# Expert layers of a fused attention, MoE and MLP kernel: 512-token slots with the second matmul two steps behind the first

## The chip, the cores and the metric

The kernel runs on one core of one Trainium2 chip. The metric is the device time of one execution in microseconds. The kernel before takes 896.44 us, the median of three runs (895.2, 896.44 and 897.1 us).

## The reference

Three layers follow one another. A gated linear attention gives 3072 tokens of 384 numbers. A mixture of experts sends each token to one of 8 experts (384 to 1024 to 384, ReLU) and scales the result by the gate weight. An MLP follows (384 to 2048 to 384, squared ReLU).

```python
# attention, for each step t
state = alpha[:, :, t, :, None] * state + einsum('bhd,bhe->bhde', k[:, :, t], v[:, :, t])
y[:, :, t] = einsum('bhd,bhde->bhe', q[:, :, t], state)
# experts; x is y as (3072, 384)
logits = x @ w_gate + modality_bias[modality_id]
e_idx = argmax(logits, axis=1)
gate_w = softmax(logits)[arange(N), e_idx]
for e in range(8):
    mask = e_idx == e
    out[mask] = gate_w[mask, None] * (maximum(x[mask] @ w1[e], 0) @ w2[e])
# MLP
r = maximum(x @ w_in, 0)
out = (r * r) @ w_out
```

All data are float32. With the reference's inputs (seed 0) two of the experts get all tokens, 1512 and 1560.

## The kernel before

**Stages.** The attention runs over 24 tiles of 128 tokens and takes the first 205 us of the span. The gate's logits, ranks and counts are computed beside it, and the scaled tokens go to DRAM (`xs`). Then come the expert layers in *slots*: a slot is 256 tokens of one expert, gathered from `xs` by an indirect DMA on GpSimd (POOL). The kernel has 13 slots, numbered 0 to 12. Slots 0 and 1 belong to the expert that leads after 16 tiles (the early slots); their token lists are ready before the others, so they cover the computing of the rest. The last stage is the MLP, in six chunks of 512 tokens and 16 steps each; it begins at 475 us.

**One matmul in three.** Every float32 product is made from three matmuls of a rounded high part and a low part (`mm3`). So every operand is split: `split` casts the high part on ScalarE (ACT, line 480) and subtracts it on VectorE (DVE, line 481). This holds for the weights, for x and for the hidden values.

```python
def mm3(o, ah, al, bh, bl, start, stop):
    PE.matmul(o, ah, bh, start=start, stop=False)
    PE.matmul(o, ah, bl, start=False, stop=False)
    PE.matmul(o, al, bh, start=False, stop=stop)
```

**A slot.** `gather` loads the tokens as two blocks of 128 rows (`xg`). `x_T` transposes them on TensorE (PE) into a PSUM tile `xt` (pool `ps_x`, one buffer) and splits that into `xh` and `xl`. `mm1(i, f)` makes one of eight 128-column blocks of the hidden layer: 9 matmuls into `hps`, then `hh` by a ReLU on ACT (line 582) and `hl` on DVE (line 583). After all eight, `mm2(i, d)` makes one of three output blocks `oo` with 24 matmuls each, and `mm2_out` copies the result into `x2T`, at an offset that is read from a register.

**Weights.** `wload` queues seven pieces of an expert: three of w1 (512 KB) and four of w2 (384 KB). At most four are in flight. `pop()` splits the oldest piece and issues the next one. There are two sets of split weights. In the loop over slots `pop()` stands behind `mm1` of f = 1, 3 and 6 and four times around `mm2`.

**w_in and w_out.** They arrive as 64-bit numbers and are converted in 24 pieces: `conv_load` (SyncE, SP), `conv_v` (five instructions on DVE, one on ACT), `conv_g` (two on POOL), `conv_store`. Pieces 0 to 11 run in the attention, 12 to 23 in slots 1 to 12, one each (two loads in slot 1).

**What sets the order.** The scheduler is off. Each engine executes in the order in which the program is written, and waits where a tile isn't ready or a buffer isn't free. An instruction that waits holds everything behind it on its engine.

**Slot assignment.** `finalize_a`, `finalize_h` and `finalize_b` compute on DVE, from the counts, the expert of each slot (`ej_i`), the place of each token (`hr`, and from it the lists `ids`) and the offsets (`eo_i`). If the slots don't suffice (`nsl_i` over `NMAIN`), the program runs a second, general path at its end (`general`), which computes everything again tile by tile.

Of the kernel before, what the change touches and what calls it, by code (L numbers as in the profile page):

```python
# [54 lines left out]
def body(ctx, tc, qka, v, alpha, mod, wg, mbias, w1, w2, w_in, w_out, out):  # L55
# [16 lines left out]
    xctx = ctx.enter_context(ExitStack())  # L72

# [11 lines left out]
    pbuf = dram.tile([NT + SL], I32, name="pbuf")  # L85
# [61 lines left out]
    ones8 = gc.tile([128, NREST], F32, name="ones8")  # L147
# [13 lines left out]
    ej_i = const.tile([128, NREST], I32, name="ej_i")  # L161
    eo_i = const.tile([128, NREST], I32, name="eo_i")
# [3 lines left out]
    def setup_gate():  # L166
# [5 lines left out]
        iota_f("slj", [128, NREST], [[1, NREST]], 0, 0)  # L172
# [5 lines left out]
        SY.dma_start(pbuf.rearrange("(o n) -> o n", n=C), raz[0][:(NT + SL) // C, 0, :C].bitcast(I32))  # L178
# [58 lines left out]
    def gate_c(g):  # L237
# [10 lines left out]
        V.tensor_scalar(rhx_all[:, t0:t0 + T, :], ri, 7, 1, op0=ALU.logical_shift_right, op1=ALU.bitwise_xor)  # L248
# [537 lines left out]
    for i in range(1, NS):  # L786
# [31 lines left out]
        if i == 1:  # L818
            x_T(i + 1, 0)
# [301 lines left out]
```

## Time and profile before

| | us |
|---|---|
| median of three runs | 896.44 |
| lowest and highest run | 895.2 and 897.1 |
| span of the profiled execution, first to last instruction | 888.7 |
| slot 2 to the end of slot 12 (251.5 to 475.2 in the span) | 223.6 |
| PE busy, share of the span | 836.7, 94% |
| VectorE busy | 551.4, 62% |
| ScalarE busy | 409.2, 46% |
| GpSimd busy | 195.3, 22% |

One execution was profiled; of its own time the span is known, 888.7 us, which is 7.7 us under the median of the runs. Rows of the profile give busy times, and the idle time of an engine with what ended it. Matmuls overlap, so the length of one (0.28 us at 256 columns) is more than the spacing of two (0.12 us); a busy PE can still be slowed. The granted clock of TensorE stands in a column of its own, 1.00 for 2.4 GHz and 0.50 for 1.2 GHz.

### The profile page before, as it was taken

Reading aid. Unit: us, or ns where it says so; the run is one execution under the profiler, and the core shown is the slowest. Engines: PE = TensorE matmul, PEld = TensorE weight load, DVE = VectorE, ACT = ScalarE, POOL = GpSimd, SP = SyncE. Lnnn points to the kernel's source line nnn. Section 1 sums busy time; section 2 is a strip of 40 time slices with the busy share of each in tenths; the row PEclk is TensorE's granted clock in tenths of the full one; section 3 lists DMA queues with packets and bytes.
Section 4 is the critical chain, followed back from the end, with each engine's and each line's share of the span. In section 5 each row is a group of like instructions: output and inputs, shape, how many; then the busy total and the mean of one; then the engine's idle time right before and its main releaser. Section 6 shows DMA issues by size and latency. Waiting matters only on the chain.

```text
span 888.7 us, 14046 instructions
## 1 busy us (share of the span) xinstructions
PE 836.7 (94%) x5424; PEld 776.9 (87%) x5424; DVE 551.4 (62%) x878; ACT 409.2 (46%) x746; POOL 195.3 (22%) x179
## 2 busy tenths in 40 slices
PE   7998889798999998989999999999999999999995
PEld 6988778698998888988988999989999999999985
DVE  7999999877577766776768634445445433333340
ACT  3655465495265554655546524324324233333331
POOL 6445355234222232322111000000000000100001
PEclk7878689699999999999999999999999999999998
DMA  9665384362496899789876300300300000000001
GB/s 247 193 195 183 114 284 145 101 224 86 130 262 212 212 210 199 204 195 196 202 199 192 104 1 18 113 1 18 112 1 19 19 1 11 26 1 18 19 1 39
DMA packets 50227, 104.59 MB, mean 118 GB/s; under 512 B 11773, under 2 KB 32279, under 8 KB 50151
## 3 DMA queue, kind: packets, MB, share of 16 engines
q1 hardware_dynamic: 46951, 93.77, 39.0%
q0 software_dynamic: 3200, 9.83, 3.1%
q8 instruction: 44, 0.72, 0.3%
q14 instruction: 32, 0.26, 0.1%
HBM read 87.83 MB, written 15.76 MB: 117 GB/s over the span
## 4 chain that ended last, share of the span: by engine, by line
PE 62%; DVE 18%; DMA 12%; issue 3%; ACT 3%; SPq 0%; POOL 0%; POOLq 0%; DVEq 0%; ACTq 0%
DMA raw<-w_dram 10%; PE h L558 8%; PE acc L559 8%; PE h L559 7%; PE acc L557 7%; PE acc L558 7%; PE h L557 7%; DVE acum L386 3%; PE oo L558 2%; PE oo L559 2%; DVE rs L390 2%; PE oo L557 2%; PE sp L412 2%; PE y L468 2%; DVE kt L394 2%
## 5 line engine op out<-in xcount | busy, mean ns | idle before, releaser
L852 DVE TENSOR_TENSOR r<-r 128x512 f32<-128x512 f32 x96 | 66.5, 693 | 147.8 <-ACT r L851 147.6
L851 ACT ACTIVATE r<-h 128x512 f32<-128x512 f32 x96 | 57.4, 598 | 160.8 <-PE h L559 159.6
L559 PE MATMUL acc<-w2h,hl 128*128 128x384 f32 x376 | 126.9, 338 | 0.0
L557 PE MATMUL acc<-w2h,hh 128*128 128x384 f32 x376 | 126.6, 337 | 0.0
L558 PE MATMUL acc<-w2l,hh 128*128 128x384 f32 x376 | 126.3, 336 | 0.0
L558 PE MATMUL h<-xl,w1h 128*128 128x512 f32 x288 | 113.9, 395 | 0.8 <-DVE xl L481 0.8
L559 PE MATMUL h<-xh,w1l 128*128 128x512 f32 x288 | 113.9, 395 | 0.0
L557 PE MATMUL h<-xh,w1h 128*128 128x512 f32 x288 | 112.1, 389 | 0.0
L875 POOL DMA_INDIRECT out_dram<-ob,pidx x24 | 24.0, 999 | 380.0 <-ACT ob L873 341.1
L481 DVE TENSOR_TENSOR hl<-r,hh 128x512 fp32r<-128x512 f32 x94 | 65.0, 692 | 64.5 <-ACT hh L480 34.3
L557 PE MATMUL oo<-hh,w2h 128*128 128x256 f32 x312 | 92.1, 295 | 7.9 <-ACT hh L582 7.9
L558 PE MATMUL oo<-hl,w2h 128*128 128x256 f32 x312 | 91.5, 293 | 7.4 <-DVE hl L583 7.3
L557 PE MATMUL hps<-xh,w1h 128*128 128x256 f32 x312 | 90.4, 290 | 3.3 <-DVE hl L583 3.3
L480 ACT CAST hh<-r 128x512 fp32r<-128x512 f32 x94 | 58.3, 620 | 75.7 <-DVE r L852 75.7
L559 PE MATMUL oo<-hh,w2l 128*128 128x256 f32 x312 | 90.4, 290 | 0.0
L558 PE MATMUL hps<-xl,w1h 128*128 128x256 f32 x312 | 88.4, 283 | 0.1
L559 PE MATMUL hps<-xh,w1l 128*128 128x256 f32 x312 | 88.2, 283 | 0.0
L481 DVE TENSOR_TENSOR w1l<-raw,w1h 128x1024 fp32r<-128x1024 f32 x42 | 51.2, 1222 | 47.5 <-ACT w1h L480 46.8
L557 PEld LDWEIGHTS acc<-w2h,hh 128*128 128x128 f32 x376 | 70.7, 188 | 4.1
L558 PEld LDWEIGHTS acc<-w2l,hh 128*128 128x128 f32 x376 | 70.6, 188 | 4.0
L559 PEld LDWEIGHTS acc<-w2h,hl 128*128 128x128 f32 x376 | 70.5, 188 | 0.2 <-DVE hl L481 0.2
L557 PEld LDWEIGHTS oo<-hh,w2h 128*128 128x128 f32 x312 | 62.0, 199 | 9.3 <-ACT hh L582 9.3
(194 smaller groups left out, 1768.1 us busy)
## 6 DMA issues: line engine op xcount, KB each, us to landing
raw<-w_dram SPq DMA_DIRECT2D x36, 512.0 KB, 10.5
raw<-w_dram SPq DMA_DIRECT2D x48, 384.0 KB, 5.7
qk<-qka_dram SPq DMA_DIRECT2D x23, 675.5 KB, 5.6
raw<-w_in_dram SPq DMA_DIRECT2D x12, 512.0 KB, 5.8
cvr<-w_out_dram SPq DMA_DIRECT2D x12, 512.0 KB, 9.7
vv<-v_dram SPq DMA_DIRECT2D x24, 192.0 KB, 5.0
xs<-xb SPq DMA_DIRECT2D x24, 192.0 KB, 3.0
alr<-alpha_dram SPq DMA_DIRECT2D x9, 512.0 KB, 4.5
```

What stands on the lines that cost most here:

```text
L386: V.tensor_tensor_scan(acum.rearrange("p a c -> p (a c)"), al, one0.rearrange("p a c -> p (a c)"), 0.0, op0=ALU.mult, op1=ALU.max)
L390: V.tensor_tensor_scan(rs.rearrange("p a c -> p (a c)")[:, ::-1], al[:, ::-1], rz.rearrange("p a c -> p (a c)")[:, ::-1], 0.0, op0=ALU.mul ...
L394: V.tensor_tensor(kt, kk, rs[:, :, 2:], op=ALU.mult)
L412: PE.matmul(sp[:, 2 * p:2 * p + 2, :], pr["kt"][:, 2 * g + p, :], pr["qb"][:, 2 * g + p], start=True, stop=True)
L480: A.copy(hi, raw)
L481: V.tensor_sub(lo, raw, hi)
L557: PE.matmul(o, ah, bh, start=start, stop=False)
L558: PE.matmul(o, ah, bl, start=False, stop=False)
L559: PE.matmul(o, al, bh, start=False, stop=stop)
L851: A.activation(r, o, AF.Relu)
L852: V.tensor_mul(r, r, r)
L875: G.indirect_dma_start(out=out, out_offset=bass.IndirectOffsetOnAxis(ap=pidx[:, n:n + 1], axis=0), in_=ob, in_offset=None)
```

## The change

Slots 0 and 1 keep 256 tokens. Slots 2 to 6 have 512 tokens, slot 7 has 256; there are 8 slots instead of 13, for the same 3328 places. An expert's remaining tokens are counted in units of 256; the first expert with an odd count has its last unit in slot 7. `x_T1` transposes one block of 128 features of a slot (four transposes for 512 tokens). `s1` and `s2` replace `mm1` and `mm2` in slots 2 to 7: step f does the first matmul of block f and the second matmul of block f - 2, which adds to three accumulators that stay open over the slot. Steps 6 and 7 of the second matmul run in the next slot. `pop()` stands behind `s1` in steps 1 to 7. Two pieces of w_out are converted in each of slots 2 to 7. `xg` has one buffer of four blocks instead of two of two, `hh` and `hl` have four buffers instead of five.

```diff
-NREST = REST // SL + NE - 1
-NMAIN = REST // SL + 1
-HC = 2 * NREST
+HC = 4 * NBIG + 2
+NSLOT = NBIG + 3
...
     def finalize_a():
...
+        V.tensor_scalar(ui, cnt, float(SL - 1), 0.0, op0=ALU.add, op1=ALU.max)
+        V.tensor_single_scalar(ui, ui, 8, op=ALU.logical_shift_right)
...
+        V.tensor_single_scalar(ui, ui, 1, op=ALU.bitwise_and)
...
+        V.scalar_tensor_tensor(small, nodd, 1.0, odd, op0=ALU.is_equal, op1=ALU.mult)
...
+        V.tensor_add(nb, u, odd)
+        V.scalar_tensor_tensor(nb, nb, 0.5, small, op0=ALU.mult, op1=ALU.subtract)
...
     def finalize_h():
...
+        V.scalar_tensor_tensor(sel, rk_all, ts, sel, op0=ALU.is_ge, op1=ALU.mult)
+        V.scalar_tensor_tensor(hr, sel, dsum, hr, op0=ALU.mult, op1=ALU.add)
         fin["hr"] = hr
...
+    def blocks(i):
+        return 2 if i < 2 or i == NSLOT - 1 else 4
...
     def gather(i):
         si = slot_ids(i)
-        xg = xp.tile([128, 2, DM], F32, tag="xg", name="xg")
-        for hf in range(2):
+        xg = xp.tile([128, 4, DM], F32, tag="xg", name="xg", bufs=1)
+        for hf in range(blocks(i)):
...
+    def x_T1(i, k):
+        n = blocks(i) * 128
+        xt = ps_x.tile([128, 512], F32, tag="x", name="xt")
+        for hf in range(blocks(i)):
+            PE.transpose(xt[:, hf * 128:(hf + 1) * 128], xgs[i][:, hf, k * 128:(k + 1) * 128], ident)
...
+        split(xt[:, :n], xh[:, :n], xl[:, :n])
...
-        pools["hp"] = pool(mctx, "hp", 5)
...
+        pools["hp"] = pool(mctx, "hp", 4)
...
+    pools["o3"] = pool(octx, "ps_o3", 1, PSUM, side="right")
...
+    drain(("w1", 0))
+    perm(1, offset(1))
+    gather(2)
+    for f in range(4, 8):
+        mm1(1, f)
+        if f == 6:
+            pop()
+    drain(("w2", 0))
+    pop()
+    mm2(1, 0)
+    pop()
+    x_T1(2, 0)
+    mm2(1, 1)
+    mm2_out(1, offset(1), 0, 2)
+    x_T1(2, 1)
+    pop()
+    mm2(1, 2)
+    x_T1(2, 2)
...
+    def s1(i, f):
...
+        for k in range(KD):
+            mm3(o, w[0][:, k, fs], w[1][:, k, fs], *xxs[i][k], k == 0, k == KD - 1)
...
+        A.activation(hh, o, AF.Relu)
+        V.scalar_tensor_tensor(hl, o, 0.0, hh, op0=ALU.max, op1=ALU.subtract)
...
+    def s2(i, f):
...
+        for d in range(KD):
+            dsl = slice(d * 128, (d + 1) * 128)
+            mm3(sac[i][d][:, :n], w[0][:, f, dsl], w[1][:, f, dsl], hh, hl, f == 0, f == 7)
+        if f == 7:
+            for d in range(KD):
+                A.copy(pools["x2T"][:, d, ds(soff[i], n)], sac[i][d][:, :n])
...
+    for i in range(2, NSLOT):
+        last = i == NSLOT - 1
+        cv = 8 + 2 * i
+        for f in range(8):
+            if f == 0:
+                if i > 2:
+                    s2(i - 1, 6)
...
+                else:
+                    gather(i + 1)
+                    push(wload(i))
+            s1(i, f)
+            if f == 1:
+                conv_load(cv)
+            if f == 2:
+                conv_load(cv + 1)
+            if f in (3, 5):
+                conv_v(cv + f // 4)
+                conv_g(cv + f // 4)
...
             if f > 0:
                 pop()
+            if f == 5:
+                if last:
+                    xx2[0] = xsplit(chunks[0], range(1))
+                else:
+                    x_T1(i + 1, 0)
+            if f == 7:
+                if last:
+                    xx2[0] = xsplit(chunks[0], range(1, KD), xx2[0])
+                else:
+                    x_T1(i + 1, 1)
+            if f == 1 and i > 2:
+                s2(i - 1, 7)
+            if f >= 2:
+                s2(i, f - 2)
+            if f == 7 and not last:
+                x_T1(i + 1, 2)
```

ACT before, from the first transposes of the next slot to the conversion in the second matmul (`hh` and `xh` are as above, `w1h` the high part of w1, `raw` a landed piece; DMAHW4 and so on are DMA completions):

```order
L480 CAST xh<-xt 128x512 [waits PE_49]
L582 ACTIVATE hh<-hps 128x256 [waits DVE_49,PE_49]
L480 CAST w1h_171<-raw 128x1024 [waits DMAHW4_49]
L582 ACTIVATE hh<-hps 128x256 [waits PE_49]
L480 CAST w1h_171<-raw 128x1024 [waits DMAHW5_49]
L480 CAST xh<-xt 128x256 [waits PE_49]
L480 CAST w1h_171<-raw 128x1024 [waits DMAHW6_49]
L627 ACTIVATE cvr<-cvr 128x512 [waits Pool_49]
```

ACT after, in slot 2, steps 3 to 5 (`cvr` is a piece of w_out):

```order
L880 ACTIVATE hh<-hps 128x512 [waits DVE_49,PE_49]
L689 ACTIVATE cvr<-cvr 128x512 [waits DMAHW0_49]
L529 CAST w1h_171<-raw 128x1024 [waits DMAHW6_49]
L880 ACTIVATE hh<-hps 128x512 [waits DVE_49,PE_49]
L529 CAST w1h_171<-raw 128x1024 [waits DMAHW7_49]
L880 ACTIVATE hh<-hps 128x512 [waits DVE_49,PE_49]
L689 ACTIVATE cvr<-cvr 128x512 [waits DMAHW2_49]
L529 CAST w1h_171<-raw 128x1024 [waits DMAHW1_49]
L529 CAST xh<-xt 128x512 [waits PE_49]
```

The casts of w1 stood around the ReLU of the last block, which the second matmul of the whole slot needs. Now each stands behind the ReLU of its own step.

PE before, in a slot, the two places where the next slot's tokens are transposed, blocks 0 and 1 of 128 features together in the first matmul, block 2 in the second one:

```order
L559 MATMUL hps<-xh,w1l_2729 128x256
L550 MATMUL xt<-ident,xg 128x128 [waits DMASW6_49,PE_49]
L550 MATMUL xt<-ident,xg 128x128 [waits DMASW7_49]
L550 MATMUL xt<-ident,xg 128x128 x2
L557 MATMUL hps<-xh,w1h_2728 128x256 [waits DVE_49]
...
L559 MATMUL oo<-hh,w2l_2731 128x256
L550 MATMUL xt<-ident,xg 128x128 [waits PE_49]
L550 MATMUL xt<-ident,xg 128x128
L557 MATMUL oo<-hh,w2h_2730 128x256
L558 MATMUL oo<-hl,w2h_2730 128x256
```

PE after, the end of a slot, from the last first-matmul of the slot to behind the transposes of block 2:

```order
L621 MATMUL hps<-xh,w1l_2765 128x512
L612 MATMUL xt<-ident,xg 128x128 [waits DVE_49]
L612 MATMUL xt<-ident,xg 128x128 x3
L619 MATMUL oo<-hh,w2h_2766 128x512 [waits Activation_49]
L620 MATMUL oo<-hl,w2h_2766 128x512
L621 MATMUL oo<-hh,w2l_2767 128x512
...
L612 MATMUL xt<-ident,xg 128x128 [waits DVE_49]
L612 MATMUL xt<-ident,xg 128x128 x3
L619 MATMUL oo<-hh,w2h_2766 128x512 [waits Activation_49]
```

The transposes of blocks 1 and 2 stood 42 matmuls apart (blocks 0 and 1 shared one tile); they now have nine matmuls between them and use the same PSUM tile.

DVE after, the last steps of the same slot (`w2l` is the low part of w2):

```order
L688 TENSOR_SCALAR cvt<-cvr 128x512 [waits DVE_49]
L530 TENSOR_TENSOR w1l_172<-raw,w1h_171 128x1024 [waits DMAHW1_49,Activation_49]
L530 TENSOR_TENSOR xl<-xt,xh 128x512 [waits Activation_49]
L881 SCALAR_TENSOR_TENSOR hl<-hps,hh 128x512 [waits Activation_49]
L530 TENSOR_TENSOR w2l_174<-raw,w2h_173 128x768 [waits DMAHW3_49,Activation_49]
L881 SCALAR_TENSOR_TENSOR hl<-hps,hh 128x512 [waits Activation_49]
L530 TENSOR_TENSOR w2l_174<-raw,w2h_173 128x768 [waits DMAHW4_49,Activation_49]
L530 TENSOR_TENSOR xl<-xt,xh 128x512 [waits Activation_49] x2
L881 SCALAR_TENSOR_TENSOR hl<-hps,hh 128x512 [waits Activation_49] x2
```

The `xl` of blocks 1 and 2 now stand together at the end, behind the `hl` and the w2 split of the last step.

## Rows read from the trace of the kernel before

**Rows 1.** Page, chain that ended last: shares of the span by line.
```profile
DMA raw<-w_dram 10%; PE h L558 8%; PE acc L559 8%; PE h L559 7%; PE acc L557 7%; PE acc L558 7%; PE h L557 7%; DVE acum L386 3%; PE oo L558 2%; PE oo L559 2%; DVE rs L390 2%; PE oo L557 2%; PE sp L412 2%; PE y L468 2%; DVE kt L394 2%
```

**Rows 2.** Windows: from:to length, busy of PE PEld DVE ACT POOL (xcount), PEclk, DMA share, GB/s.
```profile
251.54:475.16 223.62, 206.94 (x1648) 202.54 (x1647) 157.42 (x243) 124.23 (x220) 58.27 (x40) 0.98 0.85 207
```

**Rows 3.** Windows, three 256-token slots of the kernel before, in order.
```profile
311.10:331.80 20.70, 18.50 (x152) 18.09 (x152) 14.28 (x23) 11.39 (x20) 6.33 (x5) 1.00 0.95 212
331.80:354.60 22.80, 19.86 (x152) 19.46 (x151) 14.33 (x23) 11.41 (x20) 6.22 (x5) 0.93 0.91 202
354.60:372.80 18.20, 18.20 (x153) 18.08 (x152) 13.88 (x22) 11.26 (x20) 5.18 (x5) 1.00 0.86 227
```

**Rows 4.** Timeline, PE, the second of these slots: start, length, engine, line, operation [idle before].
```profile
345.45 0.38 PE L557 MATMUL oo<-hh,w2h 128*128 128x256 f32 x1 [2.01 <-ACT hh L582]
346.76 0.39 PE L558 MATMUL oo<-hl,w2h 128*128 128x256 f32 x1 [0.93 <-DVE hl L583]
```

**Rows 5.** Windows, just behind these two waits.
```profile
348.00:351.00 3.00, 3.00 (x16) 3.00 (x16) 1.67 (x3) 1.65 (x2) 0.00 (x0) 0.50 1.02 375
```

**Rows 6.** Timeline, ACT, the same place.
```profile
344.07 1.04 ACT L480 CAST w1h<-raw 128x1024 fp32r<-128x1024 f32 x1 [3.80 <-DMA raw<-w_dram]
```

**Rows 7.** Page, DMA issues: KB each, median us from issue to landing.
```profile
raw<-w_dram SPq DMA_DIRECT2D x36, 512.0 KB, 10.5
...
cvr<-w_out_dram SPq DMA_DIRECT2D x12, 512.0 KB, 9.7
...
xg<-xs,ids_b POOLq DMA_INDIRECT x2, 3.0
```

**Rows 8.** Timeline, PE: first and last of 27 unbroken 256-column matmuls.
```profile
290.42 0.28 PE L557 MATMUL hps<-xh,w1h 128*128 128x256 f32 x1
...
293.54 0.28 PE L559 MATMUL hps<-xh,w1l 128*128 128x256 f32 x1
```

**Rows 9.** Timeline, PE: nine 512-column matmuls in the last stage, first and last.
```profile
489.07 0.39 PE L557 MATMUL h<-xh,w1h 128*128 128x512 f32 x1
...
490.92 0.39 PE L559 MATMUL h<-xh,w1l 128*128 128x512 f32 x1
```

**Rows 10.** Timeline, PE, slot 1: an output block starts; later four transposes between matmuls.
```profile
245.21 0.28 PE L557 MATMUL oo<-hh,w2h 128*128 128x256 f32 x1
...
248.09 0.60 PE L550 MATMUL xt<-ident,xg 128*128 128x128 f32 x4
248.44 0.36 PE L557 MATMUL oo<-hh,w2h 128*128 128x256 f32 x1
```

**Rows 11.** Groups by line and form: xcount | busy us, mean ns.
```profile
L481 DVE TENSOR_TENSOR w2l<-raw,w2h 128x768 fp32r<-128x768 f32 x56 | 60.6, 1088 | 14.7 <-ACT w2h L480 14.4
...
L851 ACT ACTIVATE r<-h 128x512 f32<-128x512 f32 x96 | 57.4, 598 | 160.8 <-PE h L559 159.6 <-DMA wo<-cvt 0.3
...
L481 DVE TENSOR_TENSOR w1l<-raw,w1h 128x1024 fp32r<-128x1024 f32 x42 | 51.2, 1222 | 47.5 <-ACT w1h L480 46.8 <-issue 0.5
...
L481 DVE TENSOR_TENSOR xl<-xt,xh 128x512 fp32r<-128x512 f32 x13 | 9.0, 690 | 4.0 <-ACT xh L480 3.7 <-issue 0.2
```

**Rows 12.** Timeline, DVE: first and last of the five instructions of one conversion.
```profile
247.38 0.42 DVE L622 TENSOR_SCALAR cvt<-cvr 128x512 int32<-128x512 int32 x1
...
249.49 0.43 DVE L626 TENSOR_SCALAR cvt<-cvr 128x512 int32<-128x512 int32 x1
```

**Rows 13.** Timeline, DVE: a small instruction of the slot assignment, and what follows the last.
```profile
225.69 0.17 DVE L329 TENSOR_TENSOR sb<-sb,noh 128x8 f32<-128x8 f32 x1
...
230.30 0.69 DVE L481 TENSOR_TENSOR xl<-xt,xh 128x512 fp32r<-128x512 f32 x1 [1.79 <-ACT xh L480]
```

**Rows 14.** Timeline, POOL: the fourth gather behind the finished token lists.
```profile
243.25 1.59 POOL L542 DMA_INDIRECT xg<-xs,ids  x1 [0.30 <-issue]
```

**Rows 15.** Line 542, gathers started from 242 to 245 us.
```profile
DMA to landing us min/median/max: 6.2/6.9/7.7
```

**Rows 16.** Timeline, PE: where the second step of the last stage starts.
```profile
478.57 0.39 PE L557 MATMUL h<-xh,w1h 128*128 128x512 f32 x1
```

More of the change, by code (lines that the diff above doesn't have):

```diff
@@ L84, in body @@
     xs = dram.tile([NT, DM], F32, name="xs")
[L85 removed]
+    pbuf = dram.tile([NT + PAD], I32, name="pbuf")
     wi32 = dram.tile([DM, FF2], F32, name="wi32")
@@ L145, in iota_f @@
         iot[name] = f
-    ones8 = gc.tile([128, NREST], F32, name="ones8")
+    ones8 = gc.tile([128, NBIG + 1], F32, name="ones8")
     lbias = gc.tile([128, NTILE, NE], F32, name="lbias")
@@ L328, in finalize_a, with t8 @@
-        V.tensor_sub(sb, sbi, nsm)
+        def t8(tag, shape=NE, dt=F32):
+            return fp.tile([128, shape], dt, tag="f_" + tag, name=tag)
+        cnt = t8("cnt")
+        V.scalar_tensor_tensor(cnt, ohs, -2.0 * SL, run, op0=ALU.mult, op1=ALU.add)
+        ui = t8("ui", dt=I32)
+        V.tensor_scalar(ui, cnt, float(SL - 1), 0.0, op0=ALU.add, op1=ALU.max)
+        V.tensor_single_scalar(ui, ui, 8, op=ALU.logical_shift_right)
+        u = t8("u")
+        V.tensor_copy(u, ui)
+        V.tensor_single_scalar(ui, ui, 1, op=ALU.bitwise_and)
@@ new lines, in finalize_a @@
+        odd = t8("odd")
+        V.tensor_copy(odd, ui)
+        nodd = t8("nodd")
+        V.tensor_tensor_scan(nodd, ones8[:, :1].to_broadcast([128, NE]), odd, 0.0, op0=ALU.mult, op1=ALU.add)
+        small = t8("small")
+        V.scalar_tensor_tensor(small, nodd, 1.0, odd, op0=ALU.is_equal, op1=ALU.mult)
+        nb = t8("nb")
+        V.tensor_add(nb, u, odd)
+        V.scalar_tensor_tensor(nb, nb, 0.5, small, op0=ALU.mult, op1=ALU.subtract)
+        nbm = t8("nbm")
+        V.tensor_mul(nbm, nb, noh)
@@ L601, in offset @@
         if i < 2:
-            return REST + (1 - i) * SL
-        return nc.values_load(eo_i[0:1, i - 1:i], engines=[ET.SP, ET.Activation], min_val=0, max_val=REST, skip_runtime_bounds_check_because="what is left of the tokens")
+            return NT + PAD - (1 + i) * SL
+        return nc.values_load(eo_i[0:1, i - 2:i - 1], engines=[ET.SP, ET.Activation], min_val=0, max_val=NT, skip_runtime_bounds_check_because="what is left of the tokens")
     def perm(i, off):
-        SY.dma_start(pbuf[ds(off, SL)].rearrange("(h p) -> p h", p=128), slot_ids(i))
+        SY.dma_start(pbuf[ds(off, blocks(i) * 128)].rearrange("(h p) -> p h", p=128), slot_ids(i))
     cvr = {}
@@ new lines, in s2 @@
+    def s2(i, f):
+        n = blocks(i) * 128
+        if f == 0:
+            drain(("w2", i - 1))
+            sac[i] = [pools["o"].tile([128, 512], F32, tag="o", name="oo") for _ in range(2)] + [pools["o3"].tile([128, 512], F32, tag="o3", name="oo")]
+        w = w2s[(i - 1) % 2]
+        hh, hl = shh.pop((i, f))
+        for d in range(KD):
[4 more added lines that the diff above has]
+                A.copy(pools["x2T"][:, d, ds(soff[i], n)], sac[i][d][:, :n])
```

196 lines of the change are left out of this document (100 added, 96 removed).

## Prediction

> **What bounds the kernel now.** I read the chain that ended last first. Its largest single entry is not a matmul but the landing of expert weights, 10% of the span, 89 us [rows 1]. Then the windows. The expert layers from the first matmul of slot 2 to the first matmul of the last stage take 223.6 us, which is 11 slots of 256 tokens at 20.3 us, with the DMA engines 85% busy [rows 2]. The reader is to see next that the slots are not alike: one takes 18.2 us, its neighbours 20.7 and 22.8 [rows 3]. In the long ones TensorE (PE) stands twice near the middle, 2.0 us for hh from ScalarE (ACT) and 0.9 us for hl from VectorE (DVE) [rows 4]. ACT was late because the cast of a w1 piece, which stands ahead of hh in its queue, had waited 3.8 us for its DMA [rows 6]: three pieces of 512 KB and four of 384 KB are loaded in each slot, and a 512 KB piece lands 10.5 us after its issue [rows 7]. Behind the two waits the granted clock fell to 0.50 for 3 us, which is 1.2 GHz [rows 5]; so the 22.8 us slot shows 0.93. An unhindered slot is 144 matmuls of 256 columns every 0.120 us (27 in a row, 26 spacings in 3.12 us [rows 8]), 17.3 us, and six transposes, which agrees with the 18.2 us. Eleven of them would take 200 us; about 23 us of the 223.6 are waits on weights and the clock behind them. Ahead of this stretch and behind it the order on PE changes only where it is named below.
>
> **The change part by part.**
>
> Weights. Ten slots of 256 become five of 512, so five of the ten expert loads issued in them go, and a load has a slot of about 35 us instead of 20. In the ACT order the w1 casts now stand at steps 3, 4 and 5, three to four steps of 4.2 us behind their issue, against a landing of 10.5 us under the present load [rows 7]. I take the 23 us of waits as gone there. What is late next is counted below.
>
> Matmuls. Pairs of 256-column matmuls become one of 512. Their spacing is taken from the last stage: eight spacings in 1.85 us, 0.231 us [rows 9], against 2 x 0.120. Five slots have 5 x 144 = 720 of them: 166.5 us instead of 172.8. Slot 7 keeps 256 columns: 144 x 0.120 = 17.3 us. [...]
>
> The lag. The second matmul of a step now runs two steps behind the first. hh and hl of a step are needed four halves of a step, 8 us, after its first matmul ends, so ACT and DVE may be that late without PE noticing. The most that DVE gets in one step is hl, a conversion, a w1 split and an xl: 0.7 + 2.54 [rows 12] + 1.22 + 0.69 [rows 11] = 5.2 us against a step of 18 x 0.231 = 4.2 us; in the next step it has 1.8 us of work. The lag hides it: nothing. The three PSUM accumulators are freed by three ACT copies of some 0.6 us while PE does 2 us of the next slot's first matmul: nothing.
>
> Transposes. A 512-token slot needs three groups of four. A group costs 0.35 us (248.09 to 248.44) plus 0.08 for the longer first matmul behind it [rows 10], 0.43. Slots 3 to 6: 4 x 1.3 us; slot 7: 0.6. Sum 5.8 us.
>
> The new wait. At the end of each slot PE transposes feature block 1 of the next slot, does one second-matmul step (9 x 0.231 = 2.1 us) and transposes block 2 into the same single PSUM tile. This must wait until xl of block 1 is out. Ahead of that xl stand in DVE the hl of the last step and a w2 split. From the end of the first matmul: relu on ACT 0.6 us with some 0.2 us ahead of it, hl 0.7, w2 split 1.09, xl 0.69 [rows 11], about 3.3 us; PE is there after 0.4 + 2.1 = 2.5. So 0.8 us, five times: 4.0 us, bounds 0 and 1.3 each. Behind the waiting transposes stand all of PE's matmuls.
>
> The start of slot 2. Gather(2) is now four indirect loads behind the token lists, issued where before gathers 2 and 3 stood: the fourth starts at 243.25 [rows 14]. Its landing takes 3.0 us on quiet queues [rows 7] and 6.2 to 7.7 us as it was loaded here [rows 15]. It is needed earlier than before: ahead of the second output block of slot 1, which began at 245.2 [rows 10], where before the transposes stood one block later. PE waits from about 1 to 5.8 us; two 512 KB loads of w_out that shared the engines here move into slot 2, so I stay near the quiet end: 2.0. Six more transposes add 0.65. The slot assignment on DVE grows from 20 to 39 small instructions of 0.17 us ahead of xl of slot 1, of which DVE had 1.79 us spare [rows 13]: 19 x 0.17 to 0.20, less the spare, less what smaller shapes give back, delays xl by some 1.5 us and PE by 0.3 (bound 0.6), since the xl had been there early. Together 3.0 us, bounds 0.7 and 7.0.
>
> The end of slot 7. Its steps are 2.2 us, but DVE gets the same two conversions, three w1 and two w2 splits and three xl of the last stage: 2 x 2.54 + 3 x 1.22 + 2 x 1.09 + 3 x 0.69 + 5 x 0.42 for hl (the 0.42 is estimated from 0.69 for twice the size) = 15.1 us in five steps that last 10.8. The conversions also wait for their loads, 9.7 us under load [rows 7], issued 4 to 6 us ahead. The lag covers part. I take 3.5 us, bounds 0 and 6. In return the last stage no longer loses at its start: its second step began at 478.57 [rows 16], 3.4 us after its first at 475.16, where nine matmuls take 2.1: 1.3 us gained.
>
> Sum from the start of slot 2 of before: 3.0 + 166.5 + 17.3 + 5.8 + 4.0 + 3.5 = 200.1 us for 223.6, that is -23.5, and -1.3 makes -24.8. The span 888.7 becomes 863.9. The median of the runs, 896.44, is 7.7 us above this span, so I add 7.7: 871.6 us.
>
> **The rivals.** *No new waits.* If the gather lands quietly, DVE keeps up and block 2 finds its tile free, the stretch is 0.7 + 166.5 + 17.3 + 5.8 = 190.3, and the time 861.8. For it: DVE is only 70% busy now (157.4 of 223.6 [rows 2]). Against it: each wait is in the order of the program. 12%.
>
> *All bounds.* 7.0 + 166.5 + 17.3 + 5.8 + 6.5 + 6.0 = 209.1, nothing back at the start of the last stage: 881.9. The loaded landing of 7.7 us speaks for it. 8%.
>
> *The clock.* The new waits return once a slot. If each throws the clock down as in the 22.8 us slot, which took 2.1 us more than the 20.7 us one, six slots cost 12.6 us: 884.2. Against it: the 20.7 us slot had over 2 us of waits and kept 1.00 [rows 3], and the waits forecast are under 1 us. The Trainium skill (TensorE: Matmul & The Clock Gate, section Why this matters for your kernels) says that idle gaps between bursts of matmuls throw the engine back to its lower clock; the trace agrees that it can happen (0.50 [rows 5]) and that not every gap does it. 6%.
>
> *DVE becomes the bound (slower).* Place: the steps of the big slots, where hl stands behind conversions and splits. It gives a loss where DVE needs over 34.7 + 5 us a slot, since five slots have 24.8 us to lose: its work by the rows is 8 x 0.7 + 2 x 2.54 + 3 x 1.22 + 4 x 1.09 + 3 x 0.69 = 20.8 us, so it would have to double. At 45 us a slot the time is over 910. 2%.
>
> *The slots don't fit (slower).* More than five big slots sends the program into its general path as well. That path loads eight experts, 3.1 MB each, for each of 24 token tiles, 604 MB, at the 207 GB/s of the stretch [rows 2] near 2,900 us more. The reference's inputs (seed 0) put 1560 tokens on one expert and 1512 on another. After the two early slots the first has five 256-token units, the second six; the odd one goes to the small slot, and 2 + 3 = 5 fit exactly. 1%.
>
> **How the numbers follow.** The forecast has 70%, the rivals 12, 8, 6, 2 and 1, and 1% is left for a change within 0.2%, 1.8 us, about what a measurement of this kernel can tell from no change. All but the last three end faster: 0.96, same 0.01, slower 0.03. The range holds the forecast, the case without waits less 2 us for the spread of the runs, and the bounds: 859.5 to 882.
>
> **What would show it.** Right: big slots of 35 to 36 us with PE's only wait at the transposes of block 2, for xl; no wait of PE for hh; granted clock 1.00 throughout; expert loads down from 36 to 21 pieces of 512 KB; a PE wait of 1 to 3 us for the gather ahead of slot 2's first transposes; DVE busy to the end of slot 7. Wrong: spacing of the 512-column matmuls away from 0.231; casts of w1 still waiting for DMA; a wait in steps 2 to 6; a slot 7 of over 24 us; a first stage that moves by more than 2 us.

## The result, and the profile after

The kernel before ran in 895.82 us (median of four), the changed one in 870.41 (869.82 to 871.33): a ratio of 0.971, 95% interval 0.9695 to 0.9733. The forecast was 871.6 in 859.5 to 882. The time came out 1.2 us away, but not by the working: two errors of nearly 6 us cancel. The profiled execution of the changed kernel took 871.33 us with a span of 869.5; the sum had promised a span of 863.9. One execution of the kernel before (910.3 us, in the group of runs 5, 6, 7 and 9) is over 1.5% above the fastest of its group and left out of the ranges and ratios below.

First the windows of the changed kernel: from slot 2's first matmul to slot 7's, from there to the last stage, and the last stage. Columns: from and to, length, busy time of PE, its weight loads, DVE, ACT and POOL (instructions), granted clock, occupation of the DMA engines, GB/s.

```profile
257.84:429.28 171.44, 169.06 (x768) 138.30 (x767) 97.96 (x142) 72.88 (x115) 56.96 (x38) 1.00 0.65 159
429.28:457.25 27.97, 21.59 (x155) 20.77 (x154) 19.51 (x28) 13.49 (x25) 7.73 (x5) 0.88 0.68 178
457.25:869.50 412.25, 402.24 (x2019) 364.23 (x2018) 172.41 (x242) 142.62 (x242) 24.26 (x24) 0.99 0.10 31
```

The stretch from slot 2 to the last stage is 199.4 us, against 223.6 [rows 2]. Five slots of 512 tokens and most of their second matmuls take 171.4 at clock 1.00. The weak part is slot 7: PE is busy for 21.6 of 28.0 us, and the clock is 0.88. Slot 2 starts at 257.84, where in the kernel before it started at 251.54.

PE's waits in slots 2 to 6 are one row (engine, line, waited for: total, times, longest):

```profile
PE xt L612 <- DVE xl L530: 2.4, 5, 0.5
```

PE's timeline of the changed kernel has the others, and one step of 512 columns (start, length, what; in brackets the idle time ahead and what ended it):

```profile
249.95 0.47 PE L612 MATMUL xt<-ident,xg 128*128 128x128 f32 x1 [1.94 <-DMA xg<-xs,ids]
...
290.77 0.39 PE L619 MATMUL hps<-xh,w1h 128*128 128x512 f32 x1
...
292.59 0.39 PE L621 MATMUL hps<-xh,w1l 128*128 128x512 f32 x1
...
445.08 0.38 PE L620 MATMUL oo<-hl,w2h 128*128 128x256 f32 x1 [1.59 <-DVE hl L881]
...
453.45 0.58 PE L620 MATMUL oo<-hl,w2h 128*128 128x256 f32 x1 [4.79 <-DVE hl L881]
```

The reader is to see four things. No wait for hh or hl is left in slots 2 to 6. The single PSUM tile costs 2.4 us in five waits of about 0.48. The gather is waited for ahead of slot 2. And in slot 7 PE stands 1.59 and 4.79 us for hl, the second longer than anything in [rows 4]. Between 290.77 and 292.59 lie eight spacings of 512-column matmuls, 0.2275 us each, a little less than in [rows 9].

What VectorE did in slot 7 (same columns):

```profile
441.01 0.43 DVE L684 TENSOR_SCALAR cvt<-cvr 128x512 int32<-128x512 int32 x1 [3.24 <-DMA cvr<-w_out_dram]
...
444.94 2.00 DVE L530 TENSOR_TENSOR w1l<-raw,w1h 128x1024 fp32r<-128x1024 f32 x1
...
447.20 0.92 DVE L684 TENSOR_SCALAR cvt<-cvr 128x512 int32<-128x512 int32 x1
...
451.28 1.78 DVE L530 TENSOR_TENSOR xl<-x2T,xh 128x512 fp32r<-128x512 f32 x1
...
453.32 1.46 DVE L530 TENSOR_TENSOR w2l<-raw,w2h 128x768 fp32r<-128x768 f32 x1
```

And GpSimd at the same time:

```profile
443.69 2.17 POOL L695 TENSOR_TENSOR cvr<-cvr,cvt 128x512 f32<-128x512 f32 x1 [20.11 <-DVE cvt L688]
445.94 1.90 POOL L696 TENSOR_TENSOR cvt<-cvr 128x512 f32<-128x512 f32 x1
450.37 2.15 POOL L695 TENSOR_TENSOR cvr<-cvr,cvt 128x512 f32<-128x512 f32 x1 [2.53 <-ACT xh L529]
452.59 1.37 POOL L696 TENSOR_TENSOR cvt<-cvr 128x512 f32<-128x512 f32 x1
```

Piece 22 of the conversion, issued at 426.94, is there only at 441. Then the w1 split of 1.22 us [rows 11] takes 2.00, the xl of 0.69 takes 1.78, the w2 split, 0.96 us alone, takes 1.46: each begins while a GpSimd operation runs. Why piece 22 was late is in the DMA engines. The next window is the 9.7 us from the issue of slot 7's token list on:

```profile
424.50:434.20 9.70, 9.25 (x53) 7.81 (x52) 4.22 (x7) 4.64 (x10) 0.00 (x0) 1.00 0.71 42
```

They are occupied 71% and move 42 GB/s. A list is written to DRAM with 4 bytes for each token, so slot 7's takes 256 writes, and the loads issued behind it came late. Whether the list was the reason is what run 1 tries.

### The profile page after: what moved, and what is told of

Read it like the earlier page. It is cut to its first block, busy times and chain, and to the rows that moved or that the text cites. A ratio compares the mean times of both kernels' runs of the same rounds, so it can differ in the third digit from the quotient of the medians.

```text
span 869.5 us, 12270 instructions
## 1 busy us (share of the span) xinstructions
PE 819.9 (94%) x4704; PEld 733.8 (84%) x4704; DVE 508.3 (58%) x823; ACT 369.4 (42%) x663; POOL 198.9 (23%) x179
## 2 busy tenths in 40 slices
DMA packets 42542, 88.75 MB, mean 102 GB/s; under 512 B 11134, under 2 KB 26522, under 8 KB 42474
## 4 chain that ended last, share of the span: by engine, by line
PE 72%; DVE 18%; DMA 5%; ACT 2%; issue 2%; POOL 0%; SPq 0%; POOLq 0%; DVEq 0%; ACTq 0%
PE h L620 8%; PE h L621 8%; PE acc L621 8%; PE acc L619 8%; PE acc L620 8%; PE h L619 8%; PE oo L620 3%; PE hps L619 3%; PE hps L620 3%; PE oo L621 3%; PE oo L619 3%; PE hps L621 3%; DVE acum L435 3%; DVE rs L439 2%; PE y L517 2%
## 5 line engine op out<-in xcount | busy, mean ns | idle before, releaser
L620 PE MATMUL oo<-hl,w2h 128*128 128x512 f32 (+1 forms) x192 | 68.8, 358 | 6.4 <-DVE hl L881 6.4
L881 DVE SCALAR_TENSOR_TENSOR hl<-hps,hh 128x512 fp32r<-128x512 f32 (+1 forms) x48 | 30.9, 644 | 67.5 <-ACT hh L880 67.5
L619 PE MATMUL hps<-xh,w1h 128*128 128x512 f32 (+1 forms) x192 | 67.8, 353 | 2.6 <-DVE hl L645 2.6
L619 PE MATMUL oo<-hh,w2h 128*128 128x512 f32 (+1 forms) x192 | 70.1, 365 | 0.0
L621 PE MATMUL oo<-hh,w2l 128*128 128x512 f32 (+1 forms) x192 | 68.5, 357 | 0.0
L465 POOL TENSOR_SCALAR_AFFINE_SELECT pm<-pa 128x512 f32<-128x512 f32 x48 | 49.4, 1039 | 82.8 <-ACT pa L463 82.5
L620 PE MATMUL hps<-xl,w1h 128*128 128x512 f32 (+1 forms) x192 | 67.2, 350 | 0.1
L621 PE MATMUL hps<-xh,w1l 128*128 128x512 f32 (+1 forms) x192 | 67.1, 349 | 0.0
```

The costliest lines, as they stand in the source:

```text
L465: G.affine_select(out=pmt, in_=pa, pattern=[[0, 4], [1, C]], compare_op=ALU.is_ge, fill=0.0, base=0, channel_multiplier=-1)
L881: V.scalar_tensor_tensor(hl, o, 0.0, hh, op0=ALU.max, op1=ALU.subtract)
```

## Experiments

Each group ran on one chip beside the kernel before, and chips differ by some us; where a difference is under 3 us I go by the trace and not by the time.

**1. The token lists in rows (after_rows).** The list of slots 2 to 7 is transposed once on PE, and a slot writes 2 or 4 rows of 128 tokens.

```diff
+    def ids_T():
+        V.tensor_copy(ids_f, ids)
+        it = ps_x.tile([128, 512], F32, tag="x", name="it")[:HC, :128]
+        PE.transpose(it, ids_f, ident)
+        V.tensor_copy(ids_t, it)
...
     def perm(i, off):
+        if i > 1:
+            h0 = 4 * (i - 2)
+            SY.dma_start(pbuf[ds(off, blocks(i) * 128)].rearrange("(h p) -> h p", p=128), ids_t[h0:h0 + blocks(i), :])
+            return
         SY.dma_start(pbuf[ds(off, blocks(i) * 128)].rearrange("(h p) -> p h", p=128), slot_ids(i))
...
+        if f == 5:
+            ids_T()
```

> Changed kernel with one edit: the token list of slots 2 to 7 is written to pbuf in rows of 128 tokens (one PE transpose of the list in slot 1, then 4 or 2 writes of 512 B a slot) instead of 512 or 256 writes of 4 B. Theory S, the 4-byte writes hold the DMA queues: in the changed kernel the engines are 76% busy from 426 to 434 us and move 19 GB/s, right behind the list of slot 7, and conversion piece 22 lands 14 us after its issue. Then piece 22 lands in 5 to 8 us, PE's 6.4 us of waits in slot 7 fall under 2.5, and the time falls by 4 to 7 us, to 863 to 866. Theory D, the prediction's: slot 7 loses because VectorE has 15.1 us of work in steps that last 10.8. Then an earlier landing gives at most the 3.2 us that VectorE stood before piece 22, and 3 us or more of waits stay: 867 to 869. Theory V, the engines are slow because of the volume of the loads alone: no change, 869.5 to 871.5.

866.90 us (866.2 to 867.7). Windows of after_rows: the same 9.7 us behind the list, and slot 7.

```profile
422.10:431.80 9.70, 9.27 (x53) 7.83 (x52) 4.22 (x7) 4.67 (x10) 0.00 (x0) 1.00 0.56 188
...
426.87:451.52 24.65, 21.25 (x155) 20.67 (x153) 19.43 (x28) 13.57 (x25) 7.74 (x5) 0.90 0.53 170
```

PE's timeline in that slot:

```profile
447.72 0.58 PE L622 MATMUL oo<-hl,w2h 128*128 128x256 f32 x1 [3.40 <-DVE hl L895]
```

188 GB/s instead of 42, and slot 7 takes 24.65 us instead of 27.97. The conversion no longer waits for its piece. The page counts 8,244 packets under 512 bytes for 11,134: 2,890 fewer, where 2,816 list entries had been written one by one. But 3.40 us of wait for hl are left, where theory S had said under 2.5, and the time lies between the ranges of S and D. So the lists are 3.3 us of the 8.6 that slot 7 loses against the 19.33 of run 3. The time alone doesn't show the gain: against the kernel before on its own chip after_rows has a ratio of 0.973, the changed kernel 0.971.

**2. The same edit in the kernel before (before_rows).**

> Kernel before with the same single edit: lists of slots 2 to 12 written in rows of 512 B, one PE transpose more in slot 1. Theory S: the 23 us of waits and low clock in the 256-token slots come from the queues standing behind 4-byte writes (334.3 to 341.5 us: 38 GB/s at full occupation, then 318 GB/s), not from seven weight pieces a slot. Then a w1 piece lands in 5 to 7 us instead of 10.5, PE's waits for hh and hl go from 15 us to under 5, and the time falls by 12 to 20 us, to 876 to 884; most of what the larger slots brought could be had without them. Theory V, the prediction's: the volume of the loads, 85% occupation, makes the pieces late. Then the time stays within 3 us, 893 to 898.

866.30 us (863.2 to 867.3), where its unedited mate had 891.8: a ratio of 0.971, interval 0.9643 to 0.977. That is more than expected, and as much as the whole change had brought. The loads are the same 36 and 48 pieces, and again about as many small packets are gone as the lists had entries (2,970 and 2,816). ACT's waits of the kernel before from slot 2 to the last stage have this row:

```profile
ACT w1h L480 <- DMA raw<-w_dram: 28.2, 19, 3.8
```

A window of the kernel before, early in the 22.8 us slot of [rows 3]:

```profile
334.30:341.50 7.20, 7.20 (x63) 7.20 (x62) 5.19 (x10) 4.03 (x9) 2.69 (x3) 1.00 1.07 38
```

Two whole slots of before_rows, and its stretch from slot 2 to the last stage:

```profile
310.38:328.30 17.92, 17.92 (x153) 17.92 (x152) 13.80 (x23) 11.06 (x20) 5.50 (x5) 1.00 0.76 249
328.30:346.21 17.91, 17.91 (x153) 17.91 (x151) 13.79 (x23) 11.07 (x20) 5.50 (x5) 1.00 0.70 239
...
256.23:453.06 196.83, 196.75 (x1648) 196.56 (x1647) 152.02 (x242) 121.43 (x220) 55.80 (x41) 1.00 0.73 236
```

The kernel before waited 28.2 us for w1 pieces, and in one stretch of a slot its queues moved 38 GB/s at full occupation. In before_rows no cast waits for DMA, PE waits for nothing from slot 2 to the last stage, and a slot takes 17.9 us, against 18.2 to 22.8 in [rows 3]. The stretch falls from 223.6 to 196.8 us. So theory V, which is the prediction's, is wrong: twelve expert loads fit well. The 4-byte writes made them late. The Trainium skill (DMA: Bandwidth & Descriptors, section Rules for kernel authors) says that a non-contiguous last dimension becomes one descriptor per element and should be rearranged; the two runs agree, by their packets, and add what it costs here: 26.8 us of the stretch, 25.5 us of the time.

**3. Conversions out of slot 7 (conv_early).** Three pieces in each of slots 2 to 5, converted at steps 3, 5 and 7.

```diff
-        cv = 8 + 2 * i
+        cv = 6 + 3 * i
+        vg = {3: 0, 5: 1, 7: 2} if i < 6 else {}
...
+            if f in vg:
+                conv_v(cv + vg[f])
+                conv_g(cv + vg[f])
```

> Changed kernel with the twelve w_out conversion pieces in slots 2 to 5, three a slot, instead of two in each of slots 2 to 7; lists still in 4-byte writes. Theory D: VectorE's work in slot 7 falls from 15.1 to 10 us and no step waits for a conversion piece; PE's waits there go from 6.4 us to under 1.5, and the time falls by 5 to 8 us, to 862.5 to 865.5. Theory S alone: the w1 pieces of the last stage still land 9.7 us and more after their issue behind the 4-byte writes, the casts of them still stand ahead of hh on ScalarE, and 3 us or more of waits stay: 866 to 868. If three pieces a slot are too many for VectorE, new waits for hl show in slots 2 to 5 and eat the gain.

876.90 us, slower than the changed kernel. Windows of conv_early, slots 2 to 6 and slot 7:

```profile
259.46:446.15 186.69, 175.03 (x769) 142.84 (x767) 102.20 (x152) 73.76 (x117) 60.98 (x43) 0.96 0.58 156
446.15:465.48 19.33, 19.33 (x154) 18.95 (x153) 12.27 (x18) 12.26 (x22) 0.00 (x0) 1.00 0.56 179
```

One of the new waits, in its PE timeline:

```profile
330.91 1.12 PE L612 MATMUL xt<-ident,xg 128*128 128x128 f32 x4 [2.80 <-DVE xl L530]
```

Theory D had slot 7 right: 19.33 us without any wait, 8.6 less. It had the time wrong (862.5 to 865.5), since three pieces a slot did cost more than they saved, as the last sentence of the expectation allowed, but at another place than it named: PE waits for xl and not for hl. The conversion at step 7 stands ahead of xl of block 1 in VectorE's queue, so the wait for the PSUM tile grows from 0.48 to 2.8 us in four slots; behind three of these the granted clock falls (0.96 over the stretch), and slots 2 to 6 take 15.2 us more. The wait that the change had made cheap became the dearest by one badly chosen step.

**4. One step of lag (lag1).** At the slots' borders s2(i, 7) alone is left over.

```diff
-                    s2(i - 1, 6)
+                    s2(i - 1, 7)
...
-            if f == 1 and i > 2:
-                s2(i - 1, 7)
-            if f >= 2:
-                s2(i, f - 2)
+            if f >= 1:
+                s2(i, f - 1)
```

> Changed kernel with the second matmul one step behind the first instead of two. The prediction's step on the lag: hl can be 5.2 us of VectorE's work away in two steps of every slot, the lag of two steps covers it. With one step of lag hh and hl are due 2.1 us after the first matmul ends, so 2 to 3 us would be missed in two steps of each of six slots: 24 to 36 us, 894 to 906. Rival: in the trace of the changed kernel hl of the big slots is never more than 0.5 us behind its 4.1 us rhythm, since what stands ahead of it has run while PE worked, so one step is enough in the big slots and only the short steps of slot 7 lose 1 to 3 us: 870 to 874.

875.79 us. PE's waits of lag1 from slot 7 on:

```profile
PE oo L620 <- DVE hl L881: 5.1, 4, 2.0
PE oo L619 <- ACT hh L880: 2.4, 1, 2.4
```

Its slots 2 to 6 as a window:

```profile
261.56:435.03 173.47, 171.12 (x778) 139.97 (x776) 103.16 (x143) 76.01 (x118) 53.02 (x38) 1.00 0.61 158
```

None of them is in a big slot. Those take 173.47 us, which is the 171.44 of the changed kernel and the 2.05 of one second matmul (nine spacings) that now falls ahead of slot 7. Slot 7 loses 1.8 us by the same reckoning. The rest of the 5 us stands ahead of slot 2, which starts at 261.56, and is not the lag: see run 7. The time is outside both ranges and alone would have misled; in its slots the trace bears out the rival.

**5. The changed kernel again (after_again).**

> The changed kernel unaltered, as a control on the chip of this group. If chips agree: 869.5 to 871.5. The kernel before scattered from 885.9 to 896.2 in the last group while its profiled span, 888.7, lies 1.8 us under 890.5: theory R, the 4-byte lists make the loads of the 256-token slots late by a different amount each time, so before scatters and the changed kernel, whose loads have 35 us a slot, doesn't (under 3 us between its runs). Rival: the chip scatters, and the changed kernel shows as wide a spread.

871.78 us (868.8 to 873.2), the kernel before beside it 899.49 (896.7 to 907.8). In all 73 runs with a listed span the time is 1.7 to 1.9 us above it. The kernel before scattered by 7.2, 10.3 and 11.1 us within the three groups; before_rows kept within 4.2 us and the changed kernel within 4.4, where theory R had said under 3. So R has support, but it is not settled: memset_split and best2_lag1, below, scatter by 9.0 and 8.0 us. Run 7 shows one other source.

**6. Block 1 transposed half a step earlier (t2_early).**

```diff
             if f >= 2:
                 s2(i, f - 2)
-            if f == 7 and not last:
-                x_T1(i + 1, 2)
+            if f >= 6 and not last:
+                x_T1(i + 1, f - 5)
```

> Changed kernel with the transposes of block 1 of the next slot moved from behind the first matmul of step 7 to behind the second matmul of step 4, half a step earlier. Theory T, the prediction's: the only new wait in a big slot is the single PSUM tile, five times 0.48 us in the trace of the changed kernel; it goes, -2.4 us: 867.5 to 868.5. Rival: xh and xl have four buffers, so the split of block 1 waits for the first matmul of step 7 anyway, and the wait stays or moves to hl: 870 to 871.

868.54 us, 3.2 below its control. Its slots 2 to 6:

```profile
258.16:426.13 167.97, 167.97 (x768) 138.68 (x767) 98.77 (x142) 73.60 (x115) 56.91 (x38) 1.00 0.66 163
```

The slots take 167.97 us with PE busy throughout, against 171.41 in the control. The five waits are gone and each took some 0.2 us more along than its own length. The rival falls by this, and not by the times, whose ranges overlap.

**7. The memset in pieces (memset_split).** A wait of 1.7 to 4.7 us near 220 us had differed from run to run. GpSimd clears x2T there, in the changed kernel:

```profile
210.42 9.07 POOL L630 MEMSET x2T<- 128x10752 f32 x1 [8.39 <-PE y L517]
```

VectorE beside it:

```profile
215.78 0.18 DVE L228 TENSOR_TENSOR oh_all<-sc,sm 128x24 bf16<-128x24 f32 x1
...
216.09 3.42 DVE L264 TENSOR_SCALAR ss<-ss 128x3 f32<-128x3 f32 x1
```

And VectorE in lag1, where the memset ran from 210.65 to 219.72:

```profile
210.54 9.33 DVE L278 TENSOR_SCALAR bt_all<-rev,lof,tokid 128x128 f16<-128x128 f32 x2
```

VectorE's one operation on 128x3 lasts 3.42 us and ends with the memset; in lag1 two on 128x128, merged in one row, last 9.33. While the memset runs, operations with two tensor inputs pass at 0.18, as in the first row. The change itself made the memset longer, 9.07 us for 8.43, since x2T grew by 256 columns.

```diff
-        G.memset(pools["x2T"], 0.0)
+        for k in range(KD):
+            for c in range(0, NT + PAD, TB):
+                G.memset(pools["x2T"][:, k, c:c + TB], 0.0)
```

> Changed kernel with the one memset of x2T on GpSimd (9.07 us, 128x10752) cut into 21 of 128x512. In the trace of the changed kernel a VectorE operation on 128x3 takes 3.42 us and ends with that memset, in four other runs one on 128x128 takes 8.6 to 9.3 us and ends with it, and TensorE waits 1.7 to 4.7 us for hl behind it. Theory P, the two engines exclude each other on the memory for the whole of an instruction: with pieces VectorE waits at most one, about 0.5 us, TensorE's wait for hl near 220 us falls under 0.6 us, and 2 to 4 us go: 866.5 to 868.5. Rival: back-to-back pieces keep VectorE out as long as one piece does: 870 to 871.

866.68 us (863.3 to 872.3), 5.1 below its control (868.8 to 873.2), whose profiled execution had lost 4.70 us at this place. PE's wait:

```profile
220.12 0.39 PE L619 MATMUL hps<-xh,w1h 128*128 128x256 f32 x1 [0.42 <-DVE hl L647]
```

0.42 us here. But the cure isn't sure. In VectorE's timeline of best2, below, which has the pieces too, from 207.98 to 217.85, the same operation stands through several of them, as the rival has it:

```profile
213.64 4.23 DVE L266 TENSOR_SCALAR ss<-ss 128x3 f32<-128x3 f32 x1
```

And in no_pool7, below, with the memset in one piece, PE waits 0.2 us at this place. That GpSimd's instruction holds VectorE's up is shown; that pieces help is not. The Trainium skill (SBUF — State Buffer, section Who interferes with whom) describes an exclusive lock, held for a whole instruction: operations such as tensor_scalar can meet it, and those with two inputs in SBUF only against a GpSimd operation that reads SBUF, which a memset doesn't. The rows agree: 3.42 us for the tensor_scalar, 0.18 for the two-input operation ahead of it, and in slot 7 the two-input splits are held up beside GpSimd's products and sums, which read.

**8. GpSimd's two operations left out in slot 7 (no_pool7).** On top of after_rows; pieces 22 and 23 of w_out stay unfinished:

```diff
         raw, f = cvr[i]
+        if i > 21:
+            cvr[i] = f
+            return
```

> after_rows with the two GpSimd operations of conversion pieces 22 and 23 left out, so these two pieces of w_out are not finished and the output is not the reference's; VectorE's and ScalarE's work stays. In after_rows TensorE waits 3.4 us for hl in slot 7, and four VectorE operations are longer than elsewhere while GpSimd runs (w1l 2.01 for 1.22, xl 1.77 for 0.69, w2l 1.46 for 0.96, 0.93 for 0.43: 2.9 us). Theory P, GpSimd shuts VectorE out: they take their usual time, the wait falls under 1 us, and 2.5 to 4 us go: 863 to 864.5. Theory D, VectorE's own 15.1 us of work in 10.8: the wait stays at 3 us or more: 866 to 868.

861.55 us, and slot 7 falls from 24.65 to 20.70:

```profile
427.79:448.49 20.70, 19.70 (x154) 19.06 (x153) 15.55 (x27) 13.27 (x24) 0.00 (x0) 1.00 0.53 171
```

VectorE's timeline in it:

```profile
440.11 1.22 DVE L532 TENSOR_TENSOR w1l<-raw,w1h 128x1024 fp32r<-128x1024 f32 x1
...
445.16 0.68 DVE L532 TENSOR_TENSOR xl<-x2T,xh 128x512 fp32r<-128x512 f32 x1
...
446.09 0.95 DVE L532 TENSOR_TENSOR w2l<-raw,w2h 128x768 fp32r<-128x768 f32 x1
```

And PE's:

```profile
446.23 0.39 PE L622 MATMUL oo<-hl,w2h 128*128 128x256 f32 x1 [0.99 <-DVE hl L898]
```

The same splits take 1.22, 0.68 and 0.95 us, and the wait is 0.99. VectorE's work is the same as in after_rows; it was slow because GpSimd held it up. Theory P holds; theory D, the prediction's, is left with 1.4 us (20.70 against the 19.33 of conv_early). The profiled span fell further than slot 7, by 5.9 us. The last stage takes 410.1 us for 413.0. Of these 2.9 us 1.0 is PE's: behind the 3.40 us wait of after_rows the low clock reaches into the last stage (0.76 over its first 4.5 us, against 1.00 here). The other 1.9 us lie behind the last matmul, where the edit does nothing that I know of, and stay open; slot 7 starts 0.9 us later.

**9. Three edits together (best1).** Run 1's lists in rows, run 6's block 1, and run 3's conversions at other steps:

```diff
+        vg = {2: 0, 4: 1, 6: 2} if i < 6 else {}
```

> Changed kernel with three edits: lists of slots 2 to 7 in rows of 512 B (the transposed list made from the PSUM result, transposed behind step 7 of slot 1), twelve conversions as three in each of slots 2 to 5 at steps 2, 4 and 6, block 1 transposed half a step earlier. From after_rows, 866.9: less 3.4 us of wait for hl in slot 7 with the low clock behind it (1 to 1.5), less five times 0.48, less the 1.3 us for the transposed list: 858 to 860.5. If three conversions a slot put hl or xl late again, as at step 7 in conv_early (2.8 us at each slot's end), it stays at 864 or above.

860.33 us (859.3 to 860.6), inside what was expected and 11.4 below its control.

**10 and 11. Both kernels without their waits (before_clean, best2).** before_clean is before_rows with the memset in pieces. best2 is best1 with these and with the transposes for slot 2 one output block later (block 2 of them into another PSUM buffer):

```diff
-    x_T1(2, 0)
     mm2(1, 1)
     mm2_out(1, offset(1), 0, 2)
-    x_T1(2, 1)
+    x_T1(2, 0)
     pop()
     mm2(1, 2)
+    x_T1(2, 1)
     x_T1(2, 2)
```

> Kernel before with the lists of slots 2 to 12 in rows of 512 B (transposed behind step 7 of slot 1) and the x2T memset in 24 pieces. From before_rows, span 865.5: less 4.0 us of wait for hl behind the memset, less 1.0 for the transposed list, plus 1.75 from span to time: 861 to 863. Its eleven slots of 256 stay at 17.9 us each. It is the mate of best2: the difference of the two is what the larger slots bring once neither kernel waits.

> best1 with the x2T memset in 21 pieces and the transposes for slot 2 one output block later, block 2 of them in another PSUM buffer. In best1 TensorE waits 2.44 us behind the memset and 2.17 us for the gathered tokens of slot 2, with low clock behind it; both go: 853 to 857. Theory L, the larger slots have a worth of their own (720 matmuls of 512 columns at about 0.229 us instead of 1440 at 0.120, 7.9 us, less six more transposes and a longer slot assignment): 6 to 9 us below before_clean. Theory N, they only took the waits away that the 4-byte lists had made: within 2 us of before_clean.

861.30 us (857.3 to 861.7) and 852.88 (851.6 to 854.9) on one chip; the kernel before had 892.11 there, so best2 is at 0.954, interval 0.951 to 0.9577. Windows of best2, slots 2 to 6 and slot 7:

```profile
254.00:422.20 168.20, 168.16 (x769) 138.67 (x768) 107.40 (x153) 74.63 (x118) 62.14 (x43) 1.00 0.52 176
422.20:441.52 19.32, 19.32 (x154) 18.94 (x153) 12.26 (x18) 12.26 (x22) 0.00 (x0) 1.00 0.46 149
```

The slots of before_clean:

```profile
250.68:447.51 196.83, 196.76 (x1648) 196.56 (x1647) 151.89 (x242) 121.38 (x220) 55.72 (x41) 1.00 0.72 237
```

187.5 against 196.8 us, with PE busy throughout in both: the larger slots are worth 9.3 us by themselves. This is theory L. The difference in time is 8.4, and best2 beats both kernels of this case. (The profiled spans differ by 6.6 only: best2 waited 3.2 us behind the memset, before_clean 0.3.)

**12. best2 with one step of lag (best2_lag1).**

> best2 with the second matmul one step behind the first. In lag1 all waits that the shorter lag cost stood in slot 7, beside its conversions, none in the big slots. Without conversions in slot 7 ScalarE needs 0.38 and VectorE 0.42 us for hh and hl, beside a cast of 1.05 and a split of 1.22, while PE works 1.1 us: a loss of 0 to 2 us against best2 if the lag matters only there. Rival, the prediction's step that bursts of 5.2 us on VectorE need the two steps (here conversion, w1 split and hl together in step 4): waits for hl in slots 2 to 5, 6 us or more above best2.

852.05 us (847.6 to 855.6). Its slots 2 to 6 and slot 7:

```profile
254.23:424.44 170.21, 170.18 (x777) 140.40 (x776) 108.75 (x154) 77.71 (x121) 62.14 (x43) 1.00 0.52 177
424.44:441.69 17.25, 17.25 (x145) 17.25 (x144) 11.27 (x16) 10.80 (x20) 0.00 (x0) 1.00 0.46 150
```

170.21 and 17.25 sum to 187.46, as in best2. With nothing standing in slot 7, the second step of lag is worth nothing.

## Why the prediction was right in its number, step by step

The change took 24.2 us from the stretch of the slots. The runs split that into three: 26.8 us of waits and low clock that the 4-byte lists had made (223.6 to 196.8, before_rows), 9.3 us that larger slots are worth (196.8 to 187.5), and 11.9 us lost again to new waits and the clock behind them (187.5 to 199.4; 3.3 of them are the lists again, in slot 7). 26.8 + 9.3 - 11.9 = 24.2.

*Weights.* That the waits would go was right, and so were the rows: a late cast, then hh, then hl. The cause was not. The step read an occupation of 85% as volume and a landing of 10.5 us [rows 7] as the price of seven pieces. Bytes stood in the same row: 207 GB/s, when one slot of before_rows moves 249 at 76%. High occupation at low throughput was the sign, and I had not asked which descriptors stood ahead of the pieces.

*Matmuls.* 0.2275 us instead of 0.231: 720 of them are 163.8 us for 166.5. The sum was 2.7 us too high.

*The lag.* "Nothing" was right, though the reason was too generous: one step would have done in the big slots, and in slot 7 too once nothing else stood there (lag1 lost 1.8 us in slot 7, best2_lag1 nothing).

*The new wait.* A big slot takes 34.8 us from one such transpose to the next, where 35 to 36 were named as the sign. Place and mechanism of the wait were right, at 0.48 us instead of 0.8. t2_early puts all it did at 3.4 us; the step said 4.0.

*The start of slot 2.* 6.3 us instead of 3.0, the first mis-sized term. The wait for the gather was 2.3 us in three pieces for 2.0, but behind it the granted clock fell, between its levels of 1.2 and 2.4 GHz:

```profile
250.00:254.20 4.20, 4.20 (x26) 4.20 (x27) 0.69 (x1) 0.59 (x1) 0.00 (x0) 0.68 0.50 152
```

A mean of 0.68 over 4.2 us, a cost that the step had left to a rival. From the first transpose to the first matmul of slot 2 the changed kernel takes 11.2 us, the one before 6.3 for the same blocks. Another 1.4 us came from further ahead; 0.7 of it is PE's wait behind the longer memset (2.42 us for 1.74), which the step didn't see in the diff. The longer slot assignment, forecast at 0.3, shows nowhere.

*The end of slot 7.* The second mis-sized term, 5.1 us: 25.9 without the second matmul of slot 6, where 17.3 + 3.5 stood. Over 24 was among the signs that the prediction had named against itself. The work counted on VectorE (15.1 us; it was busy for 15.55 in the window of no_pool7) costs 1.4 us. What cost more was the landing behind the list (3.3 us by after_rows; the step had named the landing, at 9.7 us, and piece 22 took 14) and GpSimd (4.0 by no_pool7, with the clock), for which the step had no term.

*The start of the last stage.* 1.3 us gained, as forecast (412.25 for 413.54), and where it was forecast: the second step starts 2.2 us behind the first, for 3.4.

*The 7.7 us around the span.* Wrong, and by luck the other way. It was taken as a constant between span and time, but that is 1.7 to 1.9 us in every run. The profiled execution of before, 888.7, was a quick one (some 890.5 by that, under all four measured beside it) of a kernel that scatters by 7 to 11 us within a group. By its own execution the change is worth 19.2 us of span, where 24.8 had been forecast; against the median it is 25.4. The sum was 5.6 us too hopeful (3.3 for slot 2, 5.1 for slot 7, less 2.8 for the big slots), and the constant 5.9 too large.

*The rivals.* The mechanism of the clock rival worked at two places and not at the PSUM tile, where the wait was short; at 2.8 us, in conv_early, it worked there too, three times in four. None of the rivals held the lists, or GpSimd.

## What to carry to other kernels

Read occupation and throughput of the DMA engines together. When they are occupied and move little, look for small writes ahead of the large transfers before you change the tiling: one transpose brought what a new slot scheme brought. Subtract a kernel's profiled span only from spans, and take a term for the rest of the time from several runs. Where work moves to a place with short steps, count who else touches the same memory there.

## What the runs showed of the hardware

- A list of 256 tokens at 4 bytes took 8.3 us to land, and transfers behind it were slow: 42 GB/s at an occupation of 71% (38 at full occupation in the kernel before), 188 GB/s in the same stretch once the list was two rows of 512 bytes.
- GpSimd shuts VectorE out: splits of 1.22, 0.69 and 0.96 us took 2.00, 1.78 and 1.46 beside its two operations of a conversion, and a tensor_scalar on 128x3 lasted up to 4.2 us beside memsets. With the memset in pieces it lasted under 0.5 us in two profiled executions and 4.2 us in two others. Why is open.
- The length of one wait did not decide what the granted clock did. In the changed kernel it held through the waits of 0.5 us and through the 1.59 us in slot 7, and fell behind 1.94 and 4.79 us; but it held through the longer wait in the first row below (1.00 from 220.1 to 223.9). In conv_early it fell behind three of the four waits of 2.8 us and held behind the one in the second row (1.00 from 369.5 to 375.0).

```profile
220.09 0.39 PE L619 MATMUL hps<-xh,w1h 128*128 128x256 f32 x1 [2.42 <-DVE hl L645]
...
369.55 0.66 PE L612 MATMUL xt<-ident,xg 128*128 128x128 f32 x4 [2.81 <-DVE xl L530]
```
